# Six neighbouring rows of w_ch2 on a partition, w_ch1's columns read with a stride of six, and another margin between matmuls in the plan

## The chip, the cores and the metric

The kernel runs on one core of one Trainium2 chip. The metric is the device time of one execution in microseconds (us). TensorE (PE) does the matmuls and, on a path of its own, the weight loads (PEld); VectorE (DVE), ScalarE (ACT) and GpSimd (POOL) do the elementwise work; SyncE (SP) and POOL issue most of the DMAs. PSUM, where matmuls write, is handed out in eight banks.

## The reference

An attention with positive random features, and a token and channel mixer behind it. B = 8 batches, 8 heads, 576 tokens, head width 64, 128 features, model width 512, 256 token channels, 1536 channels.

```python
def phi(x):                                   # for q and k, both scaled by 64**-0.25
    h = einsum('bhsd,md->bhsm', x, omega) - sum(x * x) / 2
    return exp(h - max(h)) / sqrt(m)
kv, z = einsum('bhsm,bhsd->bhmd', k_p, v), sum(k_p, axis=2)
attn  = einsum('bhsm,bhmd->bhsd', q_p, kv) / (einsum('bhsm,bhm->bhs', q_p, z) + 1e-6)
x  = attn, heads side by side                 # (8, 576, 512)
u  = x + (relu(x.T @ w_tok1) @ w_tok2).T      # token mixing
out = u + relu(u @ w_ch1) @ w_ch2             # channel mixing
```

All inputs and the output are float32. w_ch1 is 512 x 1536 and w_ch2 is 1536 x 512. The sum over the 1536 channels in the last product may be taken in any order, as long as both factors use the same one.

## The kernel before, in words

All matmuls are in fp16. The 576 tokens of a batch are 512 main ones and a tail of 64; the tails of all eight batches are gathered and go through channel mixing as a ninth "batch" (c = 8).

**Stages of one batch.** The attention projects k and q on omega with matmuls of 64 contraction rows (L638, L652; the tails at L611 and its neighbours), takes exp on ACT (L514), the maximum over features on DVE (L664) and its reciprocal, scales v by it on POOL (L671, one instruction for each of four head pairs, tile vs), forms kv with 65- and 130-column matmuls (L684, L691, L693), and the numerators and denominators with 65-column matmuls (L720, L722), which DVE normalises (L729, L730) into x. Token mixing is t1 (L759, L760), a relu, and t2 (L776), whose weights are every fourth column of w_tok2; then u = x + t2 and a DMA transpose of u (L784). Channel mixing has twelve blocks of 128 channels: c1 (L854) multiplies a block of 128 columns of w_ch1 (the weights, four loads of 128x128) by u transposed, 512 tokens at a time, into one bank; a relu (L874 on ACT, L876 on DVE) puts the result into r3, channels on partitions. For batch 0 the first two blocks are split into three and one matmuls (L860, L862). c2 (L892) multiplies r3 (the weights) by w_ch2 (512 columns, the moving operand) for one fourth of the tokens at a time: twelve matmuls into one bank, issued as three jobs of four, each depending on the one before. DVE adds u (L901; a copy at L898 for batch 0, whose u comes in through 128-column identity matmuls, L890), and SP stores (L908; for the ninth batch L911 on SP and ACT).

**Loads of the weights.** w_ch1 is loaded at L444 in two halves of 768 columns: wc1 holds 128 rows on the partitions, four groups of rows, 1536 columns. w_ch2 is loaded at L459 and L460 in two halves of 768 rows: wc2[p, cb, :] is row cb*128 + p. Both convert float32 to fp16 on the way and are issued by POOL, whose DMA jobs keep the order in which they were added (`job.after`, L305). The tails of v are loaded at L345 into vt, and POOL builds from them the block-diagonal operand vbd at L596.

**The order of the work.** Nothing is issued by hand. Every piece of work is a job with an engine, an estimated cost, a key, dependencies and the buffers that it takes and gives back; the planner (class at L38, `run` at L76) lists the jobs at build time. For each engine it looks for the job that could start first in the plan, takes the smallest key among those that tie, and so fixes the order of each engine's instructions, and also which of the eight banks each job gets. The chip sees the order and semaphore waits; the planned times are not kept. The keys are batch number plus an offset from the tables KEYS (all batches), NEAR (batches 1 and 2) and HEAD (batch 0 and the loads), L17 to L19. Between a job and one that it depends on the plan leaves a margin, and on PE, when both are matmuls, a negative one, so that a matmul job may follow directly on the one it depends on:

```python
LATENCY = {"PE": 0.25, "ACT": 0.15, "DVE": 0.08, "POOL": 0.12, "SP": 0.0}   # L43
MARGIN = {"PE": 0.3, "ACT": 0.05, "DVE": 0.05, "POOL": 0.05, "SP": 0.0}      # L44
m = self.MARGIN[eng] if d.eng != eng else (-self.LATENCY["PE"] if eng == "PE" else 0.0)   # L96
```

Of the kernel before, what the change touches and what calls it, by code (L numbers as in the profile page):

```python
# [13 lines left out]
AX = mybir.AxisListType  # L14


KEYS = {"a": -1.349, "as": 0.099, "t": -1.509, "ts": 0.187, "gv": 2.165, "lt": -2.428, "lv": -3.989, "to": -2.341, "tt": 0.635, "ks": 1.094, "km": 0.303, "vs": -0.113, "l1": -0.452, "kt": -0.062}  # L17
NEAR = {"1": {"a": -1.734, "as": 0.259, "t": -2.775, "ts": 0.45, "gv": -0.056, "km": -2.03, "vs": -0.397, "kt": 0.253}, "2": {"a": -2.686, "as": 0.0, "t": -0.603, "ts": 0.324, "gv": -1.313, "km": 3.931, "vs": 0.571, "lv": -3.347, "lt": -2.872, "kt": -0.122}}
HEAD = {"kp": [-3.838, -3.822, -3.881, -3.404], "ke": [-2.728, -2.927, -2.827, -2.727], "km": [-4.039, -3.592, -4.221, -2.25], "vs": [-3.448, -3.487, -3.196, -2.472], "qp": [-3.203, -3.403, -3.303, -3.488], "qe": [-3.328, -3.374, -2.153, -3.748], "kv": [-3.407, -3.257, -2.676, -3.133], "ko": [-2.32, -3.035, -3.463, -3.168], "n": [-3.199, -3.47, -3.182, -2.377, -2.999, -3.268, -2.999, -2.899], "no": [-4.124, -3.487, -3.919, -3.144, -3.226, -3.426, -3.126, -2.386], "ktm": -3.643, "kt": -4.584, "kte": -5.022, "qt": -3.759, "qte": -5.587, "kx": [-6.213, -5.658, -5.326, -5.458], "kxo": [-6.855, -7.05, -5.723, -4.783], "ktx": -5.661, "ktxo": -5.912, "qx": [-4.987, -3.488], "qxo": [-4.073, -2.977], "qtx": -4.584, "qtxo": -3.371, "t1": [0.229, -1.008, -0.737, -0.359], "re": [0.072, -0.781, 0.181, -0.024], "ut": [0.056, -0.48, -0.104, -0.341], "uo": [-0.099, -0.259, -0.108, 0.38], "vbd": -8.41, "w1": -9.7, "w1t": -9.38, "w2t": -9.78, "wa": -8.03, "wb": -9.17, "w2": -10.08}  # L19
# [18 lines left out]
class Planner:  # L38
# [37 lines left out]
    def run(self):  # L76
# [6 lines left out]
        while any(waiting.values()):  # L83
            choice = None
            for eng, jobs in waiting.items():
                ready = []
                for j in jobs:
                    t = at[eng]
                    ok = True
                    if j.after is not None and j.after.end is None:  # L90
                        continue
                    for d in j.deps:
                        if d.end is None:
                            ok = False
# [36 lines left out]
            eng = j.eng  # L131
            waiting[eng].remove(j)
            if self.warm is not None and eng == "PE":
                if j.heavy:
                    self.warm = None
                else:
                    while t - at["PE"] > 0.3:
                        self.now = at["PE"] + 0.1
                        free = [i for i, at_ in enumerate(self.places["bank"]) if at_ < self.now]
                        if free:  # L140
                            i = min(free, key=lambda i: (self.warmed.get(i, 0), i))
                            self.warmed[i] = self.warmed.get(i, 0) + 1
                            self.warm(i)
                            last_rows = False
                        at["PE"] += 0.43 if at["PE"] < self.COLD else 0.22
                    t = max(t, at["PE"])
            self.now = t
            for tag, name in j.take:
                if (tag, name) not in self.held:
                    i = self.find(tag)[0]  # L150
                    self.places[tag][i] = math.inf
                    self.held[tag, name] = i
            cost = j.cost
            if eng == "PE":
                cost += self.SWITCH if j.rows != last_rows else 0.0
                last_rows = j.rows
            at[eng] = t + cost
            if j.wire:
                wire = max(wire, t + cost + self.BEFORE[eng]) + j.wire
                j.end = wire + self.AFTER  # L160
                lanes[eng].append(j.end)
            else:
                j.end = t + cost + self.LATENCY[eng]
            j.start = t
            j.fn()
            for g in j.give:
# [11 lines left out]
def kernel(  # L178
# [12 lines left out]
    nc = tc.nc  # L191
# [6 lines left out]
    P = 128  # L198
# [87 lines left out]
    def bank(name):  # L286
        return banks[place("bank", name)]
# [541 lines left out]
    def token_tail(pair_, key, jr, jx):  # L829
# [12 lines left out]
        j2 = add("DVE", 1.36, key, uadd, deps=[j1], give=[("bank", n), ("x", 2 * pair_), ("x", 2 * pair_ + 1)])  # L842
        return dma("SP", key + 0.02, 0.8, lambda: nc.sync.dma_start_transpose(out=uTt[:, pair_], in_=ut[pair_]), deps=[j2], cost=1.2)

    def channel_mix(c, key, jt):
        def moving(db):
            return (t_uT[place("uT", c)] if c < B else uTt)[:, :, db, :]
        jr = []
        for cb in range(NCB):
            n = ("h3", c, cb)  # L850
            def c1(cb=cb, n=n):
                ps = bank(n)
                for db in range(ND):
                    nc.tensor.matmul(ps, wc1[:, db, cb * P : (cb + 1) * P], moving(db), start=(db == 0), stop=(db == ND - 1))  # L854
# [121 lines left out]
```

## Time and profile before

| what | value |
|---|---|
| three runs | 288.77, 289.09, 289.16 us; median 289.09 us |
| the profiled execution | 289.09 us, of which the span of instructions is 287.0 us |
| PE busy | 280.2 us (98% of the span), 2186 matmuls |
| PE weight loads | 141.6 us, 2186 loads |
| DVE, ACT, POOL busy | 152.6, 153.6, 93.7 us |
| c1 weight loads (L854) | 424, mean 98 ns |
| t2 weight loads (L776) | mean 114 ns |
| matmuls of 512 columns, start to start | 216 ns |
| DMA | 39.59 MB, mean 138 GB/s |

A line of a group reads: source line, engine, operation, the tile written <- the tiles read, shape, number, then busy time in us and the mean of one in ns, and last the idle time of the engine ahead of them. A line of waits reads: who waited <- the engine, tile and line that ended the wait, then the sum in us, the number of waits and the mean. A line of the timeline reads: start and length in us, engine, line, operation and number, and in brackets the idle time ahead of it. The granted clock of TensorE was 0.998 of full speed over the span.

### The profile page before, as it was taken

How to read it: one execution, taken by the hardware profiler on the slowest of the kernel's cores; microseconds unless marked ns; L12 is line 12 of the kernel's file. 1: busy time of each engine (PE TensorE's matmuls, PEld its weight loads, DVE VectorE, ACT ScalarE, POOL GpSimd, SP SyncE). 2: the span in 40 equal slices, each digit the busy share in tenths (PEclk: the TensorE clock that was granted, in tenths of full speed). 3: DMA queues.
4: the chain of work that ended last, by engine and by line, in shares of the span. 5: the costliest groups of instructions: out<-in, count | busy, mean ns of one | idle time of the engine just before them, and what ended most of it. 6: DMA issues, size and time to landing. Idle time of an engine off the chain costs nothing.

```text
span 287.0 us, 5605 instructions
## 1 busy us (share of the span) xinstructions
PE 280.2 (98%) x2186; PEld 141.6 (49%) x2186; DVE 152.6 (53%) x330; ACT 153.6 (54%) x322; POOL 93.7 (33%) x126
## 2 busy tenths in 40 slices
PE   8999999999999999999999999999999999999994
PEld 4585554445544544454445544454455444444442
DVE  3986954546669624745584647564686331031012
ACT  2984872098449552875286537753576402602600
POOL 8994950157015701480166016601141000000000
PEclk9999999999999999999999999999999999999999
DMA  8999999999975995999989967996531042013013
GB/s 191 197 191 195 202 216 143 214 196 190 166 110 149 136 175 117 202 168 198 111 156 206 201 85 144 199 189 95 129 75 39 0 110 110 2 48 116 2 45 102
DMA packets 85721, 39.59 MB, mean 138 GB/s; under 512 B 64384, under 2 KB 80128, under 8 KB 85504
## 3 DMA queue, kind: packets, MB, share of 16 engines
q0 software_dynamic: 34288, 17.45, 44.4%
q1 hardware_dynamic: 50624, 21.01, 33.2%
q10 hardware_dynamic: 784, 0.79, 0.8%
q8 instruction: 17, 0.28, 0.4%
q14 instruction: 8, 0.07, 0.1%
HBM read 35.88 MB, written 16.52 MB: 183 GB/s over the span
## 4 chain that ended last, share of the span: by engine, by line
PE 90%; POOL 5%; DMA 3%; issue 1%; ACT 0%; DVE 0%; POOLq 0%; DVEq 0%
PE bank L892 33%; PE bank L854 32%; PE bank L776 4%; PE bank L759 4%; DMA r<-in_k_dram 3%; PE bank L638 3%; PE bank L652 3%; PE bank L684 2%; PE bank L720 2%; POOL vs L671 1%; PE bank L760 1%; POOL r L313 1%; PE bank L835 1%; PE bank L485 1%; PE bank L722 1%
## 5 line engine op out<-in xcount | busy, mean ns | idle before, releaser
L892 PE MATMUL bank<-wc,r 128*128 128x512 f16 (+2 forms) x444 | 100.7, 374 | 0.0
L874 ACT ACTIVATE r<-bank 128x512 f16<-128x512 f32 x106 | 62.7, 606 | 64.5 <-PE bank L854 64.4
L854 PE MATMUL bank<-uT,wc 128*128 128x512 f16 x376 | 88.7, 379 | 0.0
L892 PEld LDWEIGHTS <-r 128*128 128x128 f16 x444 | 40.9, 98 | 48.9 <-issue 4.4
L854 PEld LDWEIGHTS <-wc 128*128 128x128 f16 x424 | 39.7, 98 | 43.1 <-issue 0.4
L514 ACT ACTIVATE qp<-bank 128x512 f16<-128x512 f32 x64 | 35.8, 646 | 13.0 <-PE bank L652 13.0
L664 DVE TENSOR_REDUCE km<-kp 128x8 f16<-128x1024 f16 x32 | 38.5, 1202 | 2.3 <-ACT kp L514 2.3
L514 ACT ACTIVATE kp<-bank 128x512 f16<-128x512 f32 x64 | 34.6, 630 | 6.6 <-PE bank L638 6.4
L671 POOL TENSOR_TENSOR vs<-v,vs 128x512 f16<-128x512 f16 x32 | 33.3, 1063 | 13.8 <-DVE vs L666 4.3
L901 DVE TENSOR_TENSOR o<-u,bank 128x512 f32<-128x512 f16 x28 | 19.1, 683 | 34.5 <-PE bank L892 34.4
L730 DVE TENSOR_TENSOR x<-bank,rc 128x320 f16<-128x320 f32 x62 | 30.5, 492 | 2.1
L779 DVE TENSOR_TENSOR u<-x,bank 128x512 f16<-128x512 f16 x28 | 17.4, 683 | 9.5 <-PE bank L776 9.5
L729 DVE RECIPROCAL rc<-bank 128x5 f32<-128x5 f32 x62 | 11.5, 186 | 16.0 <-PE bank L722 15.8
L596 POOL TENSOR_TENSOR vbd<-vt,vbd 128x512 f16<-128x512 f16 (+1 forms) x7 | 8.2, 1173 | 35.0 <-PE bank L835 14.8
L380 POOL COPY junk<-kT 128x1 f16<-128x1 f16 x6 | 1.1, 186 | 50.5 <-DMA kT<-k 50.5
L767 DVE TENSOR_SCALAR r<-bank 128x512 f16<-128x512 f32 x7 | 4.8, 692 | 21.1 <-PE bank L760 21.1
L759 PE MATMUL bank<-x,w1m 128*128 128x512 f16 x56 | 14.4, 379 | 0.0
L720 PEld LDWEIGHTS <-qp 128*128 128x128 f16 x256 | 12.3, 98 | 4.0
L684 PEld LDWEIGHTS <-kp 128*128 128x128 f16 x256 | 11.1, 98 | 5.7 <-issue 1.1
L684 PE MATMUL bank<-vs,kp 128*128 128x65 f16 x256 | 12.9, 194 | 0.7 <-ACT r L874 0.7
L720 PE MATMUL bank<-kvsb,qp 128*128 128x65 f16 x256 | 13.5, 194 | 0.0
L776 PE MATMUL bank<-r,w 128*128 128x512 f16 x56 | 13.4, 380 | 0.0
(109 smaller groups left out, 269.5 us busy)
## 6 DMA issues: line engine op xcount, KB each, us to landing
out_dram<-o SPq DMA_DIRECT2D x32, 256.0 KB, 2.7
q<-in_q_dram POOLq DMA_DIRECT2D x6, 576.0 KB, 6.8
wc<-in_moe_w_ch_dram POOLq DMA_DIRECT2D x4, 768.0 KB, 10.6
k<-in_k_dram POOLq DMA_DIRECT2D x6, 512.0 KB, 9.1
v<-in_v_dram POOLq DMA_DIRECT2D x6, 512.0 KB, 6.7
r<-in_q_dram POOLq DMA_DIRECT2D x4, 256.0 KB, 7.2
v<-in_v_dram POOLq DMA_DIRECT2D x4, 256.0 KB, 7.1
out_dram<-o SPq DMA_DIRECT2D x5, 128.0 KB, 2.3
```

What stands on the lines that cost most here:

```text
L514: nc.scalar.activation(out=out, in_=in_, func=AF.Exp, bias=0.0, scale=1.0)
L664: nc.vector.reduce_max(out=mx, in_=kpv, axis=AX.X)
L671: nc.gpsimd.tensor_tensor(out=vs[:, :, 0:D], in0=t_v[place("v", b)][:, hh[0] : hh[0] + 2, :].rearrange("p h (j d) -> p (h j) d", d=D), in1 ...
L684: nc.tensor.matmul(ps[:, i, :], kpv[:, 2 * i + j // 2, j % 2, :], vs[:, i * NJ + j, 0 : D + 1], start=(i == 0 and j == 0), stop=False, ski ...
L720: nc.tensor.matmul(ps[:, k, j * 65 : (j + 1) * 65], st, s[:, i, 0 : D + 1], start=True, stop=True)
L730: nc.vector.tensor_tensor(out=t_x[place("x", b)][:, :, (2 * hp + hs[0]) * D : (2 * hp + hs[0] + n) * D].rearrange("p j (i d) -> p i j d", ...
L759: nc.tensor.matmul(ps, w1m[:, j, tb * P : (tb + 1) * P], x[:, j, :], start=(j == 0), stop=False)
L776: nc.tensor.matmul(ps, w2_of(tb, j), r1[:, tb, :], start=(tb == 0), stop=(tb == NT - 1))
L854: nc.tensor.matmul(ps, wc1[:, db, cb * P : (cb + 1) * P], moving(db), start=(db == 0), stop=(db == ND - 1))
L874: nc.scalar.activation(out=o, in_=bank(n), func=AF.Relu)
L892: nc.tensor.matmul(ps[:, cols], r3[:, cb, j * P : (j + 1) * P], wc2[:, cb, cols], start=(cb == 0), stop=(cb == NCB - 1))
L901: nc.vector.tensor_tensor(out=t_o[place("o", (c, j))][:, cols], in0=uu[:, cols], in1=bank(n)[:, cols], op=ALU.add)
```

## The change

Four edits, in the same file:

1. The load of each half of w_ch2 puts rows 6p to 6p+5 of the half on partition p, where it had put rows p, 128+p, 256+p and so on. A partition's six rows are then one run of 12 KB in memory and of 6 KB in the tile.
2. Slot i of half h of wc2 now holds, on partition p, channel 768h + 6p + i. So that r3 has the same channels on the same partitions, c1 takes for its block the columns 768h + i, 768h + i + 6, ... of w_ch1: a new function `wc1_block` returns that view of wc1, and the three c1 calls use it. In SBUF the 128 columns of a weight load lie 12 bytes apart, where they lay 2 bytes apart. Tile wc1 and its loads stay as they were.
3. In the planner, the margin between two jobs of PE is 0.0 in place of -0.25.
4. Some keys get other values: in KEYS ts, gv, lt, lv, km, kt; in NEAR a, ts, gv, km, kt of batch 1 and t, ts, gv, km, vs, lv, lt, kt of batch 2; in HEAD kv[1], kt, kxo[2], ktx, qtx, t1[3], ut[0] and w2t.

```diff
-KEYS = {... "ts": 0.187, "gv": 2.165, "lt": -2.428, "lv": -3.989, ... "km": 0.303, ... "kt": -0.062}
+KEYS = {... "ts": 0.07, "gv": 2.027, "lt": -1.998, "lv": -3.43, ... "km": 0.635, ... "kt": -0.125}
...
-                        m = self.MARGIN[eng] if d.eng != eng else (-self.LATENCY["PE"] if eng == "PE" else 0.0)
+                        m = self.MARGIN[eng] if d.eng != eng else 0.0
...
-            out=wc2[:, c0 : c0 + NCB // 2, :], in_=moe_w_ch2[c0 * P : (c0 + NCB // 2) * P, :].rearrange("(i p) d -> p i d", p=P))))
+            out=wc2[:, c0 : c0 + NCB // 2, :], in_=moe_w_ch2[c0 * P : (c0 + NCB // 2) * P, :].rearrange("(p i) d -> p i d", p=P))))
...
+    def wc1_block(db, cb):
+
+        n = NCB // 2
+        return wc1[:, db, (cb // n) * n * P : (cb // n + 1) * n * P].rearrange("p (c i) -> p i c", i=n)[:, cb % n, :]
...
-                    nc.tensor.matmul(ps, wc1[:, db, cb * P : (cb + 1) * P], moving(db), start=(db == 0), stop=(db == ND - 1))
+                    nc.tensor.matmul(ps, wc1_block(db, cb), moving(db), start=(db == 0), stop=(db == ND - 1))
...
-                        nc.tensor.matmul(bank(n), wc1[:, db, cb * P : (cb + 1) * P], moving(db), start=(db == 0), stop=False)
+                        nc.tensor.matmul(bank(n), wc1_block(db, cb), moving(db), start=(db == 0), stop=False)
...
-                    nc.tensor.matmul(bank(n), wc1[:, ND - 1, cb * P : (cb + 1) * P], moving(ND - 1), start=False, stop=True)
+                    nc.tensor.matmul(bank(n), wc1_block(ND - 1, cb), moving(ND - 1), start=False, stop=True)
```

In the changed file the lines behind `wc1_block` have numbers that are five higher (L854 becomes L859, L892 becomes L897).

More of the change, by code (lines that the diff above doesn't have):

```diff
@@ L14 @@
 AX = mybir.AxisListType
-KEYS = {"a": -1.349, "as": 0.099, "t": -1.509, "ts": 0.187, "gv": 2.165, "lt": -2.428, "lv": -3.989, "to": -2.341, "tt": 0.635, "ks": 1.094, "km": 0.303, "vs": -0.113, "l1": -0.452, "kt": -0.062}
-NEAR = {"1": {"a": -1.734, "as": 0.259, "t": -2.775, "ts": 0.45, "gv": -0.056, "km": -2.03, "vs": -0.397, "kt": 0.253}, "2": {"a": -2.686, "as": 0.0, "t": -0.603, "ts": 0.324, "gv": -1.313, "km": 3.931, "vs": 0.571, "lv": -3.347, "lt": -2.872, "kt": -0.122}}
-HEAD = {"kp": [-3.838, -3.822, -3.881, -3.404], "ke": [-2.728, -2.927, -2.827, -2.727], "km": [-4.039, -3.592, -4.221, -2.25], "vs": [-3.448, -3.487, -3.196, -2.472], "qp": [-3.203, -3.403, -3.303, -3.488], "qe": [-3.328, -3.374, -2.153, -3.748], "kv": [-3.407, -3.257, -2.676, -3.133], "ko": [-2.32, -3.035, -3.463, -3.168], "n": [-3.199, -3.47, -3.182, -2.377, -2.999, -3.268, -2.999, -2.899], "no": [-4.124, -3.487, -3.919, -3.144, -3.226, -3.426, -3.126, -2.386], "ktm": -3.643, "kt": -4.584, "kte": -5.022, "qt": -3.759, "qte": -5.587, "kx": [-6.213, -5.658, -5.326, -5.458], "kxo": [-6.855, -7.05, -5.723, -4.783], "ktx": -5.661, "ktxo": -5.912, "qx": [-4.987, -3.488], "qxo": [-4.073, -2.977], "qtx": -4.584, "qtxo": -3.371, "t1": [0.229, -1.008, -0.737, -0.359], "re": [0.072, -0.781, 0.181, -0.024], "ut": [0.056, -0.48, -0.104, -0.341], "uo": [-0.099, -0.259, -0.108, 0.38], "vbd": -8.41, "w1": -9.7, "w1t": -9.38, "w2t": -9.78, "wa": -8.03, "wb": -9.17, "w2": -10.08}
@@ new lines @@
+KEYS = {"a": -1.349, "as": 0.099, "t": -1.509, "ts": 0.07, "gv": 2.027, "lt": -1.998, "lv": -3.43, "to": -2.341, "tt": 0.635, "ks": 1.094, "km": 0.635, "vs": -0.113, "l1": -0.452, "kt": -0.125}
+NEAR = {"1": {"a": -1.426, "as": 0.259, "t": -2.775, "ts": 0.5, "gv": 0.127, "km": -1.859, "vs": -0.397, "kt": 0.24}, "2": {"a": -2.686, "as": 0.0, "t": -0.589, "ts": 0.371, "gv": -1.065, "km": 3.693, "vs": 0.4, "lv": -3.388, "lt": -2.446, "kt": -0.123}}
+HEAD = {"kp": [-3.838, -3.822, -3.881, -3.404], "ke": [-2.728, -2.927, -2.827, -2.727], "km": [-4.039, -3.592, -4.221, -2.25], "vs": [-3.448, -3.487, -3.196, -2.472], "qp": [-3.203, -3.403, -3.303, -3.488], "qe": [-3.328, -3.374, -2.153, -3.748], "kv": [-3.407, -3.228, -2.676, -3.133], "ko": [-2.32, -3.035, -3.463, -3.168], "n": [-3.199, -3.47, -3.182, -2.377, -2.999, -3.268, -2.999, -2.899], "no": [-4.124, -3.487, -3.919, -3.144, -3.226, -3.426, -3.126, -2.386], "ktm": -3.643, "kt": -5.305, "kte": -5.022, "qt": -3.759, "qte": -5.587, "kx": [-6.213, -5.658, -5.326, -5.458], "kxo": [-6.855, -7.05, -5.718, -4.783], "ktx": -6.15, "ktxo": -5.912, "qx": [-4.987, -3.488], "qxo": [-4.073, -2.977], "qtx": -4.567, "qtxo": -3.371, "t1": [0.229, -1.008, -0.737, -0.445], "re": [0.072, -0.781, 0.181, -0.024], "ut": [0.162, -0.48, -0.104, -0.341], "uo": [-0.099, -0.259, -0.108, 0.38], "vbd": -8.41, "w1": -9.7, "w1t": -9.38, "w2t": -8.94, "wa": -8.03, "wb": -9.17, "w2": -10.08}
```

## The prediction

> **What bounds the kernel now.** I read the busy time of each engine and the chain that ended last (page), then the busy time by stage, then what PE waited for, then the groups by shape, and last the timeline around the longest wait in mid-kernel.
>
> ```profile
> PE 280.2 (98%) x2186; PEld 141.6 (49%) x2186; DVE 152.6 (53%) x330; ACT 153.6 (54%) x322; POOL 93.7 (33%) x126
> ...
> PE 90%; POOL 5%; DMA 3%; issue 1%; ACT 0%; DVE 0%; POOLq 0%; DVEq 0%
> ```
>
> ```profile
> core 0: us, PE busy (x) PEld busy (x) DVE busy (x) ACT busy (x) POOL busy (x), PEclk, DMA share, GB/s
> 0.00:26.83 26.83, 24.83 (x294) 16.39 (x295) 18.32 (x54) 17.30 (x46) 23.95 (x36) 1.00 1.17 193
> 26.83:44.10 17.27, 16.60 (x179) 9.22 (x175) 13.43 (x31) 14.04 (x30) 10.86 (x12) 1.00 1.31 201
> 44.10:230.24 186.14, 186.14 (x1468) 91.77 (x1465) 110.55 (x231) 107.34 (x223) 58.94 (x78) 1.00 0.86 146
> 230.24:282.90 52.66, 52.66 (x257) 24.18 (x255) 10.02 (x15) 14.93 (x25) 0.00 (x0) 1.00 0.23 66
> 282.90:287.00 4.10, 0.00 (x0) 0.00 (x0) 0.29 (x1) 0.00 (x0) 0.00 (x0) 0.86 0.31 90
> ```
>
> PE carries the end: from 44.10 to 282.90 us it is busy in every nanosecond at full clock. The only room is the first 44 us and the 4.1 us behind the last matmul; anything else shortens or lengthens the kernel only through PE's own pitch.
>
> ```profile
> PE bank L943 <- DVE mask L423: 1.2, 1, 1.2
> PE bank L684 <- ACT r L874: 0.7, 1, 0.7
> PE bank L505 <- DMA r<-in_k_dram: 0.6, 1, 0.6
> PE bank L611 <- ACT qT L509: 0.2, 1, 0.2
> ```
>
> Four waits are left. Three lie ahead of the first channel matmul at 26.83 us, where both plans give PE the same order. The one at L684 is the kv of batch 1:
>
> ```profile
> 36.57 0.40 PE L684 MATMUL bank<-vs,kp 128*128 128x65 f16 x8 [0.67 <-ACT r L874]
> ```
> ```profile
> 32.27 1.94 POOL L596 TENSOR_TENSOR vbd<-vt,vbd 128x1024 f16<-128x1024 f16 x1
> 34.14 1.30 POOL L345 DMA_DIRECT2D vt<-in_v_dram  x2
> 35.45 4.09 POOL L671 TENSOR_TENSOR vs<-v,vs 128x512 f16<-128x512 f16 x4
> ```
>
> ACT is named, but it had been done; the first value scaling (L671) ended about 36.5 on POOL, behind the tail operand (L596) and two DMA issues (L345). In the single records, the kv starts 1050 ns after the last c1 matmul in place of the usual 216: a stall of 0.83 us.
>
> ```profile
> L854 PE MATMUL bank<-uT,wc 128*128 128x512 f16 x376 | 88.7, 379 | 0.0
> ...
> L854 PEld LDWEIGHTS <-wc 128*128 128x128 f16 x424 | 39.7, 98 | 43.1 <-issue 0.4
> ...
> L720 PEld LDWEIGHTS <-qp 128*128 128x128 f16 x256 | 12.3, 98 | 4.0
> L776 PEld LDWEIGHTS <-w 128*128 128x128 f16 x56 | 6.3, 114 | 5.9 <-issue 0.3
> ...
> L485 PEld LDWEIGHTS bank<-ident,wc 128*128 128x128 f32 x16 | 2.6, 187 | 0.6 <-issue 0.5
> ```
>
> These groups price a strided weight load. L854 reads columns 2 bytes apart; L720 (192 of its 256 loads) 4 bytes apart, at the same 98 ns; L776 8 bytes apart, at 114 ns. The change moves all 424 loads of c1 to 12 bytes apart.
>
> **The change part by part.** The sum is made against the profiled execution: 289.09 us, span 287.0, 2.09 around it; this is also the median of the three runs.
>
> *Matmuls.* Both orders have 2186 matmuls of the same shapes, 23 of them for warming up, and 86 changes into or out of the 64-row mode, each of which costs about 96 ns (312 against 216 from c1 to L638). Cost 0, with no cover needed: it is the same work.
>
> *Strided weight loads.* The step of 8 bytes adds 16 ns to a load. No row has 12 bytes. Between ends: nothing (as for 4 bytes), and 89 ns, the slowest load of the trace (187 ns, 4-byte elements). I take 32 ns, twice the 8-byte row's surcharge, because that row is nearest and the step from 4 to 8 bytes gave 16. Most of it is hidden: behind a 512-column matmul there are 216 ns for a load, and the t2 matmuls with 114 ns loads still follow at 216 ns. It shows where c1 follows something short. A c1 matmul now starts 29 ns behind a 65-column one, although its load has a latency of 98, so loads are pipelined and one may occupy 29 ns at most; with 32 more it occupies up to 61. In the new order the first matmul of a c1 run follows a 65-column one 13 times (32 ns each exposed), a 130-column one (58 ns pitch) 16 times (3 each), a 128-column one (56) twice (5 each). After a mode change nothing hides it (the matmul behind such a change follows at 226 to 228 ns for contiguous weights and at 243 for t2): 5 times 33. Sum 0.416 + 0.048 + 0.010 + 0.165 = 0.64 us. At no surcharge it is 0; at 89 ns it is 13 x 0.089 + 16 x 0.060 + 2 x 0.062 + 5 x 0.09 = 2.7 us.
>
> [...] No run here shows 12 bytes.
>
> *w_ch2's load.* Its rows now arrive in long runs. In the packet records of before, the two halves are 1536 packets of 1024 bytes at 98 ns; a 4096-byte packet takes 324 ns and an 18432-byte one 1377, so one of 6144 bytes takes some 486 by interpolation: 256 of them keep 16 queues for 7.8 us in place of 9.4. That is up to 1.6 us of earlier landing for what is queued behind, the k and q of batch 2. It is worth 0: k transposed lands at about 55.8 us and PE first uses it at 59.65, and PE does not wait for a DMA after the head. If that cover were gone it could give back no more than what is waited, which is 0. It cannot cost, as bytes are the same and packets fewer.
>
> *Margin and keys, first 44 us.* POOL now does the first value scaling of batch 1 ahead of the two DMA issues: 34.2 to 35.25 in place of 35.45 to 36.5. PE gets to its kv at about 35.7 and does not wait: -0.83. But the second scaling still stands behind the issues (1.30 us) and ends about 37.6, while PE is at its kv at about 36.9, as the new order puts the second kv nearer to the first: +0.67. And one c1 block of batch 0 takes a bank that a normalisation on DVE gives back about 0.2 late: +0.20. Together +0.04, with some 0.2 either way from placing times by hand. Its ends: -0.83 if neither new wait is there, and +0.9 if the old stall stays as well.
>
> *Margin and keys, 44 to 283 us.* With margin 0 the plan puts another matmul job between the three parts of a c2 group, so two groups of c2 are interleaved and each holds its bank longer. I laid the new order on the durations of before: every matmul finds its operand and bank ready. The tightest place is k's projection of batch 4, whose bank comes from an add of batch 2 with 0.42 us to spare; in before places of 0.15 us pass without a wait. Cost 0; when cover fails, a wait of 1 to 1.5 us (two adds of 0.69 us behind each other on DVE). Queues: on SP, the first store now stands behind the first three transposes (2.45, 2.71 and 4.5 us), and the last uTt transpose ahead of a store; o has four buffers at that time and no PE work waits. On POOL only the scaling is moved past L345.
>
> *Tail.* The last two adds and the last issues follow the last matmul as before: 0 to +0.03.
>
> Sum: 0.64 + 0.04 + 0 = +0.68; 289.09 + 0.68 = 289.8 us.
>
> **The rivals.**
> 1. *The strided load is hidden.* For it: loads are pipelined, and 4-byte steps cost nothing. Against: the 8-byte row, and its 17 ns behind a mode change. Time 289.09 + 0.04 = 289.1.
> 2. *Other side, faster.* POOL's earlier scaling takes the whole stall away: the second kv comes late enough on PE. Decides if PE gets to it after 37.6 us and the weight loads expose less than 0.25 us. Against it: my placing at 36.9. Time 289.09 - 0.83 + 0 to 0.2 = 288.3 to 288.5.
> 3. *A much slower load*, 187 ns: 289.09 + 2.7 + 0.04 = 291.8. For it: 12-byte steps spread a load over six times the bytes of a packed one. Against: 8-byte steps spread it over four times, for 16 ns.
> 4. *A new wait in the steady state* where interleaved c2 groups hold two banks: at the 0.42 us place or its like, 1 to 1.5 us less what shows of the strided load: 290.2 to 291.3, say 290.6. Against: no place with negative slack in my laying-out.
> 5. *The change doesn't do what it says*: w_ch2's longer packets are there, but nobody waits for them; that is part of the forecast already.
>
> **How the numbers follow.** 0.2% of 289.09, or 0.58 us, is about what a measurement of this kernel can tell from no change. Forecast (289.8, own range 289.4 to 290.2) 0.40; rival 1 0.26; rival 2 0.14; rival 3 0.08; rival 4 0.12. Range: 288.6 leaves out most of rival 2 below (0.10), 291.0 leaves out rival 3 and a little of rival 4 above (0.10). Slower: about 0.32 of the forecast's 0.40 (from 289.67 up), all of rivals 3 and 4, 0.52 together. Faster (below 288.51): rival 2 and the edge of rival 1, 0.16. Same: the rest, 0.32.
>
> **What would show it.** Weight loads of c1 at about 130 ns, 114 or less for rival 1, toward 187 for rival 3; the first c1 matmul behind a 65-column one at about 61 ns in place of 29; the wait at kv on POOL's second scaling, some 0.67 us, in place of that on the first; no other wait behind 44 us; the last matmul 0.7 us later; w_ch2 in packets over 2 KB, and no gain from them. The forecast falls if PE waits anywhere between 44 and 283 us, or if the pitch of 216 ns in a run of c1 grows: 377 such steps with some 10 ns each would be 3.8 us.

## The result, and the profile after

| | kernel before | changed kernel |
|---|---|---|
| median | 288.93 us (288.45 to 289.16, 4 runs) | 290.42 us (289.97 to 290.55, 4 runs) |
| ratio | | 1.0051, 95% interval 1.0033 to 1.0069 |
| profiled execution | 289.09, span 286.98 | 289.97, span 287.61 |
| first c1 matmul starts | 26.83 us | 26.48 us |
| from there to the start of the last matmul | 255.84 us | 256.51 us |
| from there to the end of the span | 4.31 us | 4.62 us |
| time less span | 2.11 us | 2.36 us |

The change makes the kernel 1.5 us slower by the medians (0.95 to 2.0 by the interval). The changed kernel's profiled execution happens to be the fastest of its four, 0.88 us above that of the kernel before. The lower half of the table divides those 0.88 us: -0.35 + 0.67 + 0.31 + 0.25. The first of these is within chance: in the kernels below that wait for nothing more there, the first c1 matmul starts anywhere from 26.36 to 27.04 us, with the same matmuls ahead of it. Without it the span would be 0.98 us longer, which is nearer to the medians of the spans: 287.9 us, against 286.9 to 287.1 in the series of the kernel before that ran beside the experiments.

Busy times and the chain by engine, from the page of the changed kernel:

```profile
PE 280.3 (97%) x2186; PEld 152.1 (53%) x2186; DVE 152.0 (53%) x330; ACT 153.7 (53%) x322; POOL 93.0 (32%) x126
...
PE 89%; POOL 6%; DMA 3%; issue 1%; DVE 0%; POOLq 0%; DVEq 0%
```

PE is busy for as long as before and waits for more; its weight loads take 10.5 us more in all. What PE waited for (us in total, times, longest):

```profile
PE bank L948 <- DVE mask L423: 1.2, 1, 1.2
PE bank L865 <- DMA wc<-in_moe_w_ch_dram: 0.9, 1, 0.9
PE bank L485 <- DMA wc<-in_k_dram: 0.7, 1, 0.7
PE bank L611 <- ACT qT L509: 0.2, 1, 0.2
```

The wait at the first kv of batch 1 (L684) is gone, and a wait that nobody had forecast is there: the first c1 job (L865) waits for a load of w_ch1. The timeline of PE around it, first in the kernel before, then in the changed one:

```profile
26.83 1.47 PE L860 MATMUL bank<-uT,wc 128*128 128x512 f16 x6
```

```profile
26.48 0.42 PE L865 MATMUL bank<-uT,wc 128*128 128x512 f16 x1
27.78 1.28 PE L865 MATMUL bank<-uT,wc 128*128 128x512 f16 x5 [0.88 <-DMA wc<-in_moe_w_ch_dram]
```

One matmul goes, and the next, on the same half of w_ch1, starts 1.30 us later in place of 0.216: 1.08 us lost. The DMA that it waits for is the load of the *second* half, issued by POOL at 19.14 us; its landing, 8.6 us later, is the 27.7 us at which PE goes on. Nothing that this job computes needs the second half. In the trace the job's second weight load holds a semaphore wait that it doesn't hold in the kernel before. The weight loads, by shape:

```profile
L859 PEld LDWEIGHTS <-wc 128*128 128x128 f16 x424 | 50.7, 126 | 33.1 <-issue 0.2
...
L776 PEld LDWEIGHTS <-w 128*128 128x128 f16 x56 | 6.3, 114 | 5.8 <-issue 0.3
```

The loads of c1, 12 bytes apart, take 126 ns against 98. POOL's timeline around batch 1's value scalings:

```profile
32.08 1.94 POOL L596 TENSOR_TENSOR vbd<-vt,vbd 128x1024 f16<-128x1024 f16 x1
33.97 1.06 POOL L671 TENSOR_TENSOR vs<-v,vs 128x512 f16<-128x512 f16 x1
34.97 1.30 POOL L345 DMA_DIRECT2D vt<-in_v_dram  x2
36.27 3.09 POOL L671 TENSOR_TENSOR vs<-v,vs 128x512 f16<-128x512 f16 x3
```

The first scaling has moved ahead of the two issues, as the built order said. The second ends at 37.35, and PE comes to its kv only at 37.56, because of the 1.08 us lost earlier. Finally the last issues, first of the kernel before, then of the changed kernel (DMA issues on the queues of SP and ACT):

```profile
282.90 1.11 SPq L911 DMA_DIRECT2D out_dram<-o  x2
282.91 1.38 ACTq L911 DMA_DIRECT2D out_dram<-o  x2
```
```profile
282.64 1.75 SPq L916 DMA_DIRECT2D out_dram<-o  x3
282.65 2.04 ACTq L916 DMA_DIRECT2D out_dram<-o  x3
```

Before, two issues are left on each queue; now three stand in a row, right behind one another. The third ends only some 0.08 us later behind the last matmul's start than the second did before (1.41 us in place of 1.33 on SP, 1.70 in place of 1.61 on ACT). What changes more is the work of the DMA engines. Two stretches of each kernel, from 0.50 us ahead of the last matmul's start to 0.55 behind it and from 0.85 to 2.00 behind it (the last two columns are the busy share of the DMA engines and GB/s), first of the kernel before:

```profile
282.18:283.23 1.05, 0.71 (x13) 0.54 (x10) 0.78 (x2) 0.00 (x0) 0.00 (x0) 1.00 0.89 242
283.52:284.68 1.16, 0.00 (x0) 0.00 (x0) 0.00 (x0) 0.00 (x0) 0.00 (x0) 1.00 0.51 128
```
```profile
282.49:283.54 1.05, 0.72 (x13) 0.55 (x10) 0.90 (x3) 0.00 (x0) 0.00 (x0) 1.00 0.00 0
283.84:284.99 1.15, 0.00 (x0) 0.00 (x0) 0.00 (x0) 0.00 (x0) 0.00 (x0) 1.00 0.97 281
```

Before, the store of the last group but one goes out while PE is still at work; now the DMA engines stand idle there, and that store takes them up when the two parts of the last group's store want them.

Where the 0.67 us on PE between the first c1 matmul and the last come from, by start-to-start intervals: +1.08 for the new wait, -0.83 for the old one, +0.34 for strided loads, +0.10 ahead of a numerator of batch 1 (130 ns behind L722 in place of 29), -0.02 left over. The strided loads show in two places. In 12 runs of c1 behind a 65-column matmul the second interval is 233 ns in place of 216 (before, 221 in three of them): 0.19 us. In four places behind a mode change (into or out of matmuls of 64 rows), and once behind the new wait, it is 256 ns in place of 226: 0.15 us. Between 44 us and the end PE has no wait, though pairs of c2 groups now alternate.

### The profile page after: what moved, and what is told of

Read it like the earlier page. It is cut to its first block, busy times and chain, and to the rows that moved or that the text cites. A ratio compares the mean times of both kernels' runs of the same rounds, so it can differ in the third digit from the quotient of the medians.

```text
span 287.6 us, 5598 instructions
## 1 busy us (share of the span) xinstructions
PE 280.3 (97%) x2186; PEld 152.1 (53%) x2186; DVE 152.0 (53%) x330; ACT 153.7 (53%) x322; POOL 93.0 (32%) x126
## 4 chain that ended last, share of the span: by engine, by line
PE 89%; POOL 6%; DMA 3%; issue 1%; DVE 0%; POOLq 0%; DVEq 0%
PE bank L897 33%; PE bank L859 32%; PE bank L776 4%; PE bank L759 4%; DMA wc<-in_moe_w_ch_dram 3%; PE bank L652 3%; PE bank L720 2%; PE bank L684 2%; PE bank L638 2%; POOL vs L671 1%; PE bank L760 1%; POOL vt L345 1%; POOL r L313 1%; PE bank L835 1%; POOL r L324 1%
## 5 line engine op out<-in xcount | busy, mean ns | idle before, releaser
L879 ACT ACTIVATE r<-bank 128x512 f16<-128x512 f32 x106 | 63.7, 609 | 73.0 <-PE bank L859 72.2
L897 PE MATMUL bank<-wc,r 128*128 128x512 f16 (+2 forms) x444 | 101.5, 374 | 0.0
L859 PE MATMUL bank<-uT,wc 128*128 128x512 f16 x376 | 89.8, 380 | 0.0
L859 PEld LDWEIGHTS <-wc 128*128 128x128 f16 x424 | 50.7, 126 | 33.1 <-issue 0.2
L897 PEld LDWEIGHTS <-r 128*128 128x128 f16 x444 | 40.6, 98 | 47.5 <-issue 4.7
L720 PEld LDWEIGHTS <-qp 128*128 128x128 f16 x256 | 12.8, 98 | 5.1 <-issue 0.4
L720 PE MATMUL bank<-kvsb,qp 128*128 128x65 f16 x256 | 14.1, 193 | 0.0
L684 PEld LDWEIGHTS <-kp 128*128 128x128 f16 x256 | 10.9, 98 | 4.1 <-issue 0.6
L684 PE MATMUL bank<-vs,kp 128*128 128x65 f16 x256 | 13.0, 193 | 0.0
## 6 DMA issues: line engine op xcount, KB each, us to landing
wc<-in_moe_w_ch_dram POOLq DMA_DIRECT2D x4, 768.0 KB, 10.5
```

The lines of the kernel that those rows point to most:

```text
L684: nc.tensor.matmul(ps[:, i, :], kpv[:, 2 * i + j // 2, j % 2, :], vs[:, i * NJ + j, 0 : D + 1], start=(i == 0 and j == 0), stop=False, ski ...
L720: nc.tensor.matmul(ps[:, k, j * 65 : (j + 1) * 65], st, s[:, i, 0 : D + 1], start=True, stop=True)
L859: nc.tensor.matmul(ps, wc1_block(db, cb), moving(db), start=(db == 0), stop=(db == ND - 1))
L879: nc.scalar.activation(out=o, in_=bank(n), func=AF.Relu)
L897: nc.tensor.matmul(ps[:, cols], r3[:, cb, j * P : (j + 1) * P], wc2[:, cb, cols], start=(cb == 0), stop=(cb == NCB - 1))
```

## The experiments

**First group: which part of the change costs what.** Two theories. W: the strided view makes the first c1 job wait for w_ch1's second half, and strided loads show 0.35 us. K: the time comes with the margin and the keys, the layout is hidden.

*Halves of w_ch1 apart in the tile, in the changed kernel.* The view of a half then spans no address of the other.

```diff
-    wc1 = sb([P, ND, DC], FP16, "wc1")
+    wc1 = sb([P, 2, ND, DC // 2], FP16, "wc1")
...
-            out=wc1[:, :, c0 : c0 + DC // 2], in_=moe_w_ch1[:, c0 : c0 + DC // 2].rearrange("(i p) c -> p i c", p=P))))
+            out=wc1[:, i], in_=moe_w_ch1[:, c0 : c0 + DC // 2].rearrange("(i p) c -> p i c", p=P))))
...
-        return wc1[:, db, (cb // n) * n * P : (cb // n + 1) * n * P].rearrange("p (c i) -> p i c", i=n)[:, cb % n, :]
+        return wc1[:, cb // n, db].rearrange("p (c i) -> p i c", i=n)[:, cb % n, :]
```

> The changed kernel with w_ch1's two halves apart in the tile (a partition holds half 0 whole, then half 1), everything else as in the changed kernel, so the strided columns of half 0 no longer span addresses of half 1. Theory W (the strided columns make the first c1 matmuls wait for the load of the second half of w_ch1; 1.08 us in the changed kernel's trace): the wait on that DMA is gone from the first c1 job. PE then reaches the kv of batch 1 some 0.7 us earlier than in the changed kernel, so the wait for POOL's second value scaling (0.67 us forecast) and for a bank (0.20) can come back. Time 0.2 to 1.1 us below the changed kernel: 0.2 if both waits come back whole, 1.1 if neither does. Rival K (the extra time comes from the new margin and keys, the layout being hidden): the same time as the changed kernel, within 0.15 us.

Measured: 290.31 us (289.88 to 290.77, 6 runs), ratio to the kernel before 1.0049 (1.0036 to 1.0062): 0.11 us below the changed kernel. The time alone would fit K. The trace does not: the wait on the DMA is gone, and this one, in PE's timeline, has taken its place:

```profile
37.74 0.40 PE L684 MATMUL bank<-vs,kp 128*128 128x65 f16 x8 [0.92 <-POOL vs L671]
```

That is the second kv of batch 1 behind POOL's second scaling (1301 ns in place of 216: 1.08 us). There are 0.23 us ahead of a c1 block too, where the kernel before has 0.14. The gain is below W's lower end of 0.2 us, but by W's mechanism: both forecast waits come back, somewhat larger. The stage is paced by POOL, and the earlier wait of 1.08 us on PE costs no more than those 0.11 us on top.

*The layout alone, on the kernel before.*

```diff
-            out=wc2[:, c0 : c0 + NCB // 2, :], in_=moe_w_ch2[c0 * P : (c0 + NCB // 2) * P, :].rearrange("(i p) d -> p i d", p=P))))
+            out=wc2[:, c0 : c0 + NCB // 2, :], in_=moe_w_ch2[c0 * P : (c0 + NCB // 2) * P, :].rearrange("(p i) d -> p i d", p=P))))
...
+    def wc1_block(db, cb):
...
-                    nc.tensor.matmul(ps, wc1[:, db, cb * P : (cb + 1) * P], moving(db), start=(db == 0), stop=(db == ND - 1))
+                    nc.tensor.matmul(ps, wc1_block(db, cb), moving(db), start=(db == 0), stop=(db == ND - 1))
...
```

> The kernel before with the layout alone: six neighbouring rows of w_ch2 on a partition, w_ch1's columns with a stride of six; margin and keys as before. Theory W: the first c1 job waits for the second half of w_ch1 (about 0.95 us, from 26.83 to 27.78), the wait of 0.83 us at the kv of batch 1 disappears behind it, since PE comes there 0.95 us later, and strided weight loads show 0.35 us: 0.95 - 0.83 + 0.35 = +0.5 us against the kernel before (0.3 to 0.8). Rival K: within 0.15 us of the kernel before.

Measured: 290.03 us (289.61 to 290.38, 5 runs), ratio 1.0038 (1.0025 to 1.0051): +1.0 us, above the range. In its trace the first c1 job waits (1149 ns in place of 216, for the second half), the old wait at kv is gone, and the strided loads show 0.33 us. But there is also a wait that belongs to neither, at 126 us, here on PE and on POOL:

```profile
126.49 0.40 PE L684 MATMUL bank<-vs,kp 128*128 128x65 f16 x8 [0.97 <-POOL vs L671]
```
```profile
120.83 0.19 POOL L386 COPY junk<-uT 128x1 f16<-128x1 f16 x1 [2.89 <-DMA uT<-u]
...
124.11 1.25 POOL L345 DMA_DIRECT2D vt<-in_v_dram  x2
125.37 2.08 POOL L671 TENSOR_TENSOR vs<-v,vs 128x512 f16<-128x512 f16 x2
```

POOL waited for a transpose of u to land (120.8 us; in the kernel before 119.5, with its scaling at 124.03), issued six loads behind it (four of them left out above), and came late with the scaling.

*The same with the halves apart.* Both edits together.

> The kernel before with the layout, and w_ch1's halves apart in the tile, so that only the strided weight loads and the longer runs of w_ch2 are left. Theory W: no wait on the second half's DMA at the first c1 job, the wait of 0.8 us at the kv of batch 1 as in the kernel before, c1 weight loads of 126 ns, and +0.35 us (0.2 to 0.5) against the kernel before. Rival K: 0, within 0.15 us. If the longer runs of w_ch2 bring anything, the time is below the kernel before.

Measured: 289.07 us (288.71 to 289.66, 11 runs) against 288.99 in the same series, ratio 1.0004 (0.9994 to 1.0015): +0.08 us, with -0.17 to +0.43 inside the interval. The trace has loads of 126 ns, 0.33 us more of small delays, and no wait for w_ch1. The old wait at the first kv is there (0.75 us), and 0.24 us of a wait at 126 us. The time neither shows nor excludes the 0.35.

*The new margin, keys and order with the plain layout.*

```diff
-            out=wc2[:, c0 : c0 + NCB // 2, :], in_=moe_w_ch2[c0 * P : (c0 + NCB // 2) * P, :].rearrange("(p i) d -> p i d", p=P))))
+            out=wc2[:, c0 : c0 + NCB // 2, :], in_=moe_w_ch2[c0 * P : (c0 + NCB // 2) * P, :].rearrange("(i p) d -> p i d", p=P))))
...
-        return wc1[:, db, (cb // n) * n * P : (cb // n + 1) * n * P].rearrange("p (c i) -> p i c", i=n)[:, cb % n, :]
+        return wc1[:, db, cb * P : (cb + 1) * P]
```

> The changed kernel with its margin, keys and order, but w_ch2 and w_ch1's columns as in the kernel before. Theory W: the DMA wait (1.08 us) and the strided loads (0.35) are gone, the wait for POOL's second value scaling (0.67) and for a bank (0.20) show: 0.5 us below the changed kernel if both come whole, 1.4 if neither does, so +0.1 to +1.0 us against the kernel before. Rival K: the same time as the changed kernel, +1.4 us against the kernel before.

Measured: 289.67 us (289.16 to 290.31, 10 runs), ratio 1.0022 (1.0012 to 1.0033): +0.68 us (0.35 to 0.95). Inside W's range, yet not for W's reason. In its trace the second kv of batch 1 waits 0.32 us and a c1 block 0.23, less together than the 0.83 and 0.14 of the kernel before, and its last matmul starts 0.18 us *earlier* than in the kernel before. What it loses lies behind the last matmul: 4.63 us to the end of the span in place of 4.31, as in the other two kernels with this order (4.62, 4.62). And time less span is 2.43 us in the median of its runs (four of the ten at 2.04 to 2.12, the others at 2.41 to 2.61), where that of the kernel before is 2.02. K holds for this part: about half of the change's cost has nothing to do with w_ch1 or w_ch2.

**Second group: the end, the margin, POOL, and the layout again.**

*The old margin for the ninth batch's c2 alone, on the last kernel.*

```diff
-        self.heavy = False
+        self.heavy = self.chain = False
...
-                        m = self.MARGIN[eng] if d.eng != eng else 0.0
+                        m = self.MARGIN[eng] if d.eng != eng else (-self.LATENCY["PE"] if j.chain else 0.0)
...
-                               deps=[prev, *jr[4 * part : 4 * part + 4], *j_wc2], take=[("bank", n)], give=[("r3", c)] + ([("uT", c)] if c == 0 else []))
+                               deps=[prev, *jr[4 * part : 4 * part + 4], *j_wc2], take=[("bank", n)], give=[("r3", c)] + ([("uT", c)] if c == 0 else [])); prev.chain = c == B
```

> The changed kernel's margin, keys and order with the plain layout (the run of +0.68 us), except that the old margin of -0.25 stays for the c2 jobs of the ninth batch, so that its last groups are no longer interleaved; nothing else moves. Theory T (in the new order the add and the stores of the last but one group come right ahead of the last two, and queue the last issues on ACT and SP): the time from the last matmul's start to the end of the span falls from 4.63 to the 4.31 us of the kernel before, and the time by 0.3 us, to +0.35 against the kernel before. Should the 0.4 us that the kernels with the new order have more around their spans hang on the same stores, it goes too, and the time is within 0.1 us of the kernel before. Rival (the end is longer for another reason): 4.63 stays, +0.68 us.

Measured: 289.47 us (288.85 to 291.39, 11 runs), ratio 1.0014 (0.9997 to 1.003): +0.44 us, which the intervals don't tell from the +0.68 without this edit; POOL's wait at kv was 0.84 us in this trace and 0.32 in that one. The trace shows the end by itself: from the last matmul's start it takes 4.09 us, less than in the kernel before. Its last issues, from the timeline:

```profile
283.10 1.11 SPq L916 DMA_DIRECT2D out_dram<-o  x2
283.10 1.38 ACTq L916 DMA_DIRECT2D out_dram<-o  x2
```

Two on each queue again. The records tell why 4.09 and not 4.31: SP has seen all stores land 3.25 us behind the last matmul's start (3.26 in the kernel before, 3.78 in the changed one), so the interleaved end cost 0.52 us by the landing, not 0.31; but DVE's last drain starts 3.96 us behind it in the kernel before and 3.59 here, and the other engines go on only behind that drain (in the kernel before it ends at 4.09 us, POOL goes on at 4.13, SP and ACT at 4.25). Theory T holds for its cause, the interleaved order, which is the only thing that this edit takes away. It doesn't hold for its means: the queue of issues makes the last issue some 0.08 us later, and the rest of the 0.52 is transfers. Here the DMA engines are busy for 0.89 of the stretch around the last matmul's start and 0.50 of the one behind it, as in the kernel before. The time less span stayed at 2.47 us: it does not hang on the stores.

*The margin alone, on the kernel before,* L96 with 0.0 as in the change, keys as before.

> The kernel before with the margin of 0 between matmul jobs alone; keys and layout as before. If the margin makes the new order's extra time (the end of the span 0.32 us longer, 0.4 us more around it): +0.3 to +0.8 us against the kernel before, with 4.6 us behind the last matmul's start. If the keys make it: within 0.15 us of the kernel before. New waits of the interleaved c2 groups would show as waits for a bank or an add on DVE behind 44 us; I expect none.

Measured: 291.33 us (290.82 to 291.65, 5 runs), ratio 1.0075 (1.006 to 1.009): +2.2 us (1.7 to 2.6), far above the expected 0.3 to 0.8. Of the 1.94 us that its profiled span is longer, 0.84 lie behind the last matmul (5.15 us); the row of issues is there, and the stores are seen landed only at 4.32. On PE there are 66 changes into or out of the 64-row mode where the kernel before has 62, an interval of 465 ns between two 64-row matmuls at 62 us with a delay of 0.18 us behind it, and a delay of 0.22 us at 70 us; the old wait at kv stayed (0.81). So the margin by itself is costly, and with it the changed keys win back about 1.5 us (+2.2 against +0.68). No run has the keys without the margin.

*POOL's two issues behind all four scalings, on the kernel before.* The job's place in the plan is kept and only its emission is moved, so that no other engine's order changes.

```diff
-    ld = {}
+    ld, late = {}, []
...
-            jobs.append(dma("POOL", key + 0.01 * g, 0.22 if b < NPE else 0.4, tails, take=[("vt", b)], deps=deps, cost=0.7))
+            jobs.append(dma("POOL", key + 0.01 * g, 0.22 if b < NPE else 0.4, (lambda tails=tails: late.append(tails)) if b == NPE else tails, take=[("vt", b)], deps=deps, cost=0.7))
...
                     in1=vs[:, :, D : D + 1].broadcast_to((P, 8, D)),
                     op=ALU.mult,
-                )
+                ); [go() for go in late if (b, hp) == (1, 3)]
```

> The kernel before with POOL's two issues of v's tail (batch 2) behind all four value scalings of batch 1; no other engine's order moves. If POOL sets the pace of the kv stage of batch 1, the wait of 0.83 us at its first kv goes and no other takes its place: 0.83 us below the kernel before. If another wait is right behind it (a normalisation on DVE, a relu), 0.2 to 0.6 us below. If the stage was bound by something else: the same time.

Measured: 288.61 us (288.08 to 290.31, 12 runs) against 289.03, ratio 0.9986 (0.9966 to 1.0005). All that PE still waits for, from its waits, lies ahead of the first c1 matmul:

```profile
PE bank L943 <- DVE mask L423: 1.2, 1, 1.2
PE bank L611 <- ACT qT L509: 0.2, 1, 0.2
```

The median span fell by 0.75 us (286.9 to 286.15), nearly the 0.83. The time less span rose by 0.36 (2.08 to 2.44), so that half of it doesn't reach the time, and the interval of the time alone does not show a gain.

*The layout alone, a second time.*

> The layout alone on the kernel before, once more, for a second trace. The first had little left of the wait for w_ch1's second half (POOL's chain had come 0.3 us earlier and hid it) and a wait of 1.13 us at a kv of batch 4 at 125 us, for POOL's value scaling, which was late as POOL had waited for a DMA transpose. If that wait comes from the layout, it is there again, and the time again +1.0 us; if it is chance in the DMA's timing, it is absent or elsewhere, and the time about +0.5 us by the strided loads and what POOL leaves of the first wait.

Measured: 289.57 us (288.99 to 290.16, 10 runs), ratio 1.0017 (1.0005 to 1.0029): +0.54 us. The trace has the wait on w_ch1's second half (1175 ns in place of 216), none at 126 us, and none at a kv of batch 1; its last matmul starts within 0.03 us of that of the kernel before. This profiled execution is one of the fastest of its ten (span 287.0, median 287.5). The wait at 126 us is thus no fixed part of the layout: it came with the landing of a transpose. Whether the layout makes a late landing likelier is not shown. The medians of both series say that the layout as written costs more than with the halves apart.

**Third group: a faster version, and the price of a step.**

*The new order with the old margin for the ninth batch, the plain layout and POOL's issues moved.* The edits of the fifth and seventh runs together.

> The changed kernel's margin, keys and order with the plain layout and the old margin for the ninth batch (289.47 us), and with POOL's two issues of v's tail behind all four value scalings of batch 1; no other engine's order moves. If POOL's chain bounds the kv stage of batch 1 in the new order too, its wait (0.84 us in that kernel's trace) goes: 288.6 us, 0.4 below the kernel before; the wait of 0.23 us ahead of a c1 block (a bank that a normalisation on DVE gives back) stays. Rival: the stage is bound by DVE's normalisations or ACT's relus, and the wait moves there: 289.3 to 289.5.

Measured: 288.54 us (287.6 to 289.41, and the profiled execution with 292.74; 12 runs) against 289.12, ratio 0.9976 (0.9963 to 0.9989): 0.6 us faster than the kernel before, and as forecast. It beats both kernels. In the profiled execution PE waited 2.2 us for a load of k, and the first c1 matmul came at 30.09 us, so the stage is read in the next.

*The same with the change's layout,* halves apart.

> The same with the change's layout (six neighbouring rows of w_ch2, w_ch1 read with a stride of six, its halves apart in the tile): the change without its wait on w_ch1's second half, without its longer end and without POOL's wait. The strided loads alone are left against the run beside it: +0.35 us (0.2 to 0.5) by the trace of the changed kernel (12 x 17 ns behind a 65-column matmul, 5 x 30 ns behind a mode change). Rival: longer runs of w_ch2 bring transfers forward, and the two are the same within 0.15 us.

Measured: 288.81 us (288.35 to 291.26, 11 runs), ratio to the kernel before 1.0003 (0.9986 to 1.0019): by the medians 0.27 us above the run beside it, where 0.35 was expected; the two intervals overlap in part, so this is agreement in size and not a proof. No wait at kv is left in its trace, and 4.11 us lie behind the last matmul.

*Other steps.* w_ch2 with three and with two neighbouring rows on a partition (steps of 6 and 4 bytes in w_ch1), and with twelve (24 bytes). Of each edit, the view alone:

```diff
...
+        n = (3, 2)[cb // 6]
+        return wc1[:, cb // 6, db].rearrange("p (g c i) -> p g i c", c=P, i=n)[:, cb % 6 // n, cb % n, :]
...
```

```diff
...
+        n = NCB
+        return wc1[:, db].rearrange("p (c i) -> p i c", i=n)[:, cb, :]
...
```

> The kernel before with other steps, the halves of w_ch1 apart: three neighbouring rows of w_ch2 on a partition in half 0 (w_ch1's columns 6 bytes apart), two in half 1 (4 bytes apart); the two halves' c1 matmuls have lines of their own. Loads seen so far: 98 ns at 2 and 4 bytes, 114 at 8, 126 at 12. If the surcharge grows with the step beyond 4 bytes: 106 ns at 6 bytes, 98 at 4. If it sets in only at 8: 98 at both. The time is that of the kernel before, within what one run tells.

> The layout alone on the kernel before with twelve rows of w_ch2 on a partition, w_ch1's columns 24 bytes apart over its whole width (so the wait for its second half is real here). [...] The time is 0.3 to 1 us above the kernel before.

Measured, in the groups by shape: first 4 and 6 bytes, then 24.

```profile
L862 PEld LDWEIGHTS <-wc 128*128 128x128 f16 x216 | 20.4, 98 | 23.0 <-issue 0.4
L860 PEld LDWEIGHTS <-wc 128*128 128x128 f16 x208 | 20.4, 103 | 19.2
```
```profile
L859 PEld LDWEIGHTS <-wc 128*128 128x128 f16 x424 | 57.6, 143 | 27.8 <-issue 0.4
```

At 4 bytes 98 ns, at 6 bytes 103, at 24 bytes 143, with times of 289.04 and 289.88 us (one run each). So a load takes 98, 98, 103, 114, 126 and 143 ns at steps of 2, 4, 6, 8, 12 and 24 bytes. (The 8-byte row is t2's, from another tile.) From 4 to 12 bytes a straight line through the two ends, 98 and 126 ns, or 3.5 ns a byte, gives 105 and 112 ns at 6 and 8, within 2 ns of the 103 and 114 measured. It doesn't go on: at 24 bytes the line would give 168 ns, and an end of the growth at 12 bytes 126, and the load takes 143, or 1.4 ns a byte beyond 12. Nor does it begin before 4 bytes: at 2 bytes a load takes 98 ns too. This is a fit and not a mechanism shown. Where nothing hides it, the 24-byte step costs some 30 ns behind a 65-column matmul and 54 in place of 10 behind a mode change (17 and 40 at 12 bytes), and 5 ns behind a 130-column one, where 12 bytes cost nothing.

Time less span, medians, for the kernels above:

| kernel | us |
|---|---|
| before (three series) | 2.02, 2.08, 2.05 |
| layout alone (twice); halves apart; margin alone | 2.03, 2.05; 2.06; 1.93 |
| the change; halves apart; plain layout; old margin at the end | 2.52; 2.51; 2.43; 2.47 |
| before with POOL's issues moved | 2.44 |
| the last two kernels of the third group | 2.47, 2.44 |

## Why the prediction was right

It said 289.8 us, 288.6 to 291.0, with slower the likeliest; 290.42 is inside. The sign and the range were right. The size was not: +1.5 us by the medians against +0.68, beyond the forecast's own 289.4 to 290.2. Its main term was right in kind and half as large; a wait was missing, and the step on the tail failed. That the time still lies in the whole range is partly luck.

- **Matmuls: 0.** Right: 2186 matmuls, 62 mode changes behind the first c1 matmul in both traces.
- **Strided weight loads: +0.64.** Right in mechanism, nearly twice too large. The load takes 126 ns, near the forecast 130. But 32 ns each behind a 65-column matmul were 17, in the second interval and not in the first, which stayed at 29 ns where the prediction looked for 61; the 130-column places cost nothing; the mode changes cost 30 each (33 forecast). Sum 0.34 us in the trace. In the three pairs of runs that differ by the layout alone, halves apart, it is 0.08, 0.27 and 0.64 us slower (289.07 against 288.99, 288.81 against 288.54, 290.31 against 289.67; in the last POOL's wait differs too). The rival that hides the load whole is refuted by the trace, as is rival 3 with its 187 ns; no single time does it.
- **What the step changed besides its price.** This was missed. The prediction priced the strided read and never asked what the read *depends* on. The view of a block with a step of six, from the second group of rows on, was taken to overlap the load of the other half, and the wait is in the built program: the second weight load of the first c1 job carries a wait for the second load. Putting the halves apart removed it. On the kernel before it costs: +1.0 and +0.5 us with it, +0.1 without. In the changed kernel it is worth almost nothing (290.42 against 290.31), as POOL's wait would stand behind it.
- **w_ch2's longer runs: 0.** Right: 1280 packets fewer, packets of 6144 bytes at 474 ns in the median (the prediction's 486 was to be an interpolation, which gives 474). The loads of w_ch2 land no sooner, 12.8 us behind the issue in place of 12.7 (medians of two), and none of the three pairs above is faster with the layout.
- **Margin and keys, first 44 us: -0.83 + 0.67 + 0.20 = +0.04.** Right in its parts, where they can be seen. The old wait is gone at the first kv. The one at the second kv was hidden in the changed kernel by the wait for w_ch1, and was 0.32, 0.84 and 1.08 us in three kernels with this order and without that wait; the spread follows POOL's chain, which in the changed kernel's trace starts, at 31.51 us, behind a wait of 0.49 us for a load of v. The bank's wait was 0.23 us ahead of the c1 block in those three, where the kernel before has 0.14; in the changed kernel it stayed at 0.13, with 0.10 ahead of a numerator.
- **Rival 2, POOL's stall goes wholly.** It needed PE to come after 37.6 us, when the second scaling was to end. PE came at 37.56, behind its end at 37.35, and did not wait; but what made it late cost more (1.08) than the rival gained.
- **Margin and keys, 44 to 283 us: 0.** Right for the changed kernel, where no wait shows. So rival 4, into whose times 290.42 falls, is not what happened. It would have been wrong without the keys: the margin alone makes +2.2 us.
- **Tail: 0 to +0.03.** This step failed. It looked at the last two adds and issues, which do follow the last matmul as before, and not at what goes ahead of them: interleaving brings the add and the store of the group before to the same place, three issues stand on ACT and SP, and their transfers share the DMA engines, which had been idle (busy for 0.00 of the stretch ahead and 0.97 of the one behind, where the kernel before has 0.89 and 0.51). 0.52 us by the landing of the stores, 0.31 in the span, as the end of the program behind that landing took 0.84 us in place of 1.05.
- **Around the span: taken over as 2.09.** It became 2.5, and that is 0.4 of the 1.5 us. The runs show that it is not the margin (1.93 with it alone) and not the layout, and that moving two of POOL's issues is enough to cause it in the kernel before. That the changed kernel, in which a scaling also goes ahead of these issues, has it for the same reason is not shown. What it is lies outside the trace and stays open.

So the forecast of +0.68 and the 0.88 us of the profiled pair are different sums: 0.64 + 0.04 there, 0.34 (loads) + 0.35 (1.08 - 0.83 + 0.10, the first stage) + 0.31 (end) + 0.25 (around) - 0.35 (an earlier first c1 matmul, within what such starts vary) - 0.02 here. That the two lie near each other is luck: an overestimate at the loads and an early first c1 matmul stand against what was left out.

## What to carry to other kernels

When an operand's access pattern changes, read the waits of the built program as well as the order of its instructions: a strided view can be taken to overlap with a transfer that it doesn't touch (1.08 us at the first c1 job here), and laying the tile out so that each transfer owns one contiguous stretch removed the wait (on the kernel before, +0.08 us in place of +1.0 and +0.5). Before pricing a wait that goes, look for the engine that paces the stage: here it was POOL, and both a wait added on PE (1.08 us) and one taken away (0.83) disappeared behind it, until two DMA issues (1.30 us together) were moved on POOL itself. At the end of a kernel, ask what else the DMA engines still have to move when the last stores are issued, and whether it could have gone out earlier; don't look at the last issue alone.

## What the runs showed of the hardware that was not expected

- A weight load of 128x128 in fp16 slows with its column step gradually: 98, 98, 103, 114, 126, 143 ns at 2, 4, 6, 8, 12, 24 bytes; where c1 follows a t1, t2 or c2 matmul of 512 columns, none of the 12-byte step's surcharge shows (215 to 216 ns, start to start, in the traces of both kernels). From 4 to 12 bytes the growth is 3.5 ns a byte, to within 2 ns, and from 12 to 24 bytes 1.4.
- Behind a 65-column matmul the extra load time shows in the second interval, and smaller than the load grew (17 of 28 ns at 12 bytes).
- The time around the span takes values near 2.05 and near 2.45 us, and the order of POOL's instructions alone can move it: 1.86 to 2.16 us in all 73 runs of the kernel before, 2.28 to 2.52 in all twelve with two issues of POOL moved. Other kernels show both values, one in one run and one in another.
- Three stores that end together cost 0.52 us more until they had landed than two, while the last issue came only some 0.08 us later: the DMA engines were busy for 0.97 of the stretch in place of 0.51.
- The first c1 matmul started anywhere from 26.36 to 27.04 us in kernels with the same matmuls ahead of it (leaving out the 30.09 us above and the 24-byte step, which needs both halves), and a transpose's landing moved by 1.3 us from one kernel to another and cost 1.1 us at 126 us. A difference of 0.3 us in one trace against another can therefore be chance, unless it sits at a place that the change touches.
